# New costs and due times for a list scheduler that orders one stage of a kernel

## The chip, the cores and the metric

The kernel runs on one NeuronCore of a Trainium2 chip. Five instruction streams work side by side and meet only at semaphores: PE (TensorE, matrix products), DVE (VectorE), ACT (ScalarE), POOL (GpSimd) and SP (SyncE, which here only issues DMA transfers). Each engine takes its own instructions strictly in the order in which the program holds them. The metric is the device time of one execution in microseconds (us), median of several; lower is better.

## The reference

Three layers in a row, all in fp32 (shapes: 2 batches, 8 heads, 768 tokens, 64 wide; then 1536 tokens of 512).

```python
# attention, for each of the 16 (batch, head) pairs
q_bucket = sum(((q @ proj) > 0) * powers)        # 6 sign bits
k_bucket = sum(((k @ proj) > 0) * powers)
scores = where(q_bucket[:, None] == k_bucket[None, :], 0.125 * q @ k.T, -1e9)
attn = exp(scores - max(scores))
x = (attn / (attn.sum(-1) + 1e-9)) @ v
# dense layer: 512 -> 2048 -> 512 with mish, weights given in fp64
h = x @ w_in;  x = (h * tanh(softplus(h))) @ w_out
# eight experts: 512 -> 1024 -> 512 with relu, weighted by a Sinkhorn-normalised gate
out = sum_e P[:, e] * (relu(x @ w1[e]) @ w2[e])
```

## The kernel before, in words

**Stages.** `attention()` comes first, and then the two feed-forward layers as one long loop over 240 steps of matrix products. The change touches only `attention()`. To keep fp32 accuracy at the fast fp32r rate, operands are split into a high part (the fp32r rounding) and a low part (value minus high part), and products are sums of two or three fp32r products.

**Units of attention.** There are 16 heads `h`, each with two query blocks `u` (32 in all, 384 queries each). For one query block:

- `s_mm` (PE, tile `ps`, L369): three score tiles of 128 queries by 768 keys, with the bucket bits inside the product; `s_max` (DVE, `mx<-ps`, L383) takes each row's maximum. Only one `ps` buffer exists, so product and maximum alternate. `cols` (DVE, L388 and L391), `rows_mm` (PE, `prow`, L404) and `rows_cp` (ACT, `row`, L413) turn the maxima into rows that SP copies into place.
- For six key chunks `c`: `st_mm` (PE, `pst`, L421 and L422) makes transposed scores, `st_exp` (ACT, `p`, L427) their exponentials. Four of the six chunks are split: `split_hi` (`ph<-p`, through `copy`, L430) on ACT or DVE, `split_lo` (`plo<-p,ph`, through `subtract`, L433) on POOL. `av_mm` (PE, `pav`, L471) multiplies with the values; `av_count` (PE, `pav<-..,vf`, L456) opens each block's sum, so its row marks the start of a block's last part.
- `av_out` moves the sums out of PSUM (DVE `rs`, L479; ACT `xu`, L481). `norm` divides in five parts: reciprocals on DVE (L490, L493, L495), part 3 the product (`xu<-xu,rs`, L500, DVE), part 4 the high part (`xh`, L430), part 5 the low part (`xl`, L433).

For each head, `load_qk` and `load_v` bring data in, `prep_hi`, `prep_lo` and `prep_move` split it and SP moves the halves into the sets `sq`, `zq`, `ak`, `bk` (one of the three sets lies in the tile `wx`), `bits_*` (L306 to L327) make the bucket bits, `bits_fin` (`bit<-bit,cst`, L327, DVE) scales them.

**Decoding.** Between these, attention decodes the first four of the sixteen fp64 weight blocks, two chunks of 512 KB each: SP loads a chunk into a `stage` tile (three buffers, L105), then nine parts turn the fp64 bits into fp32 (DVE L119, L121, L127, L131, L135, L139; ACT L123, L125; POOL L141; DVE or POOL L143). `weight_hi` and `weight_lo` (L155, L160) split three finished blocks; the fourth is split when the feed-forward loop begins.

**What sets the order.** All of attention is a list of tasks. A task has an engine or a choice of engines with a cost each (`"A.42|D.27"`: ACT at 0.42 us or DVE at 0.27 us), a due time, and the tasks it comes after. When the program is built, a greedy list scheduler (the loop at the end of `attention()`) keeps a clock for each engine, takes the task with the least `start + DELTA * due`, and emits it. The costs and due times so decide the order on each engine and the engine of every task with a choice; at run time semaphores decide when anything starts. Chunk `n` of the decoding has the due time `DUE0 + PACE * n`, and a query block has `6 * u`.

Of the kernel before, what the change touches and what calls it, by code (L numbers as in the profile page):

```python
# [16 lines left out]
P = 128  # L17
B, H, S, D = 2, 8, 768, 64
# [4 lines left out]
E = 8  # L23
# [8 lines left out]
NSTAGE = 3  # L32
# [3 lines left out]
NP = 5  # L36
NPH = 3
WARM = 8
DELTA = 0.012
RECEIPT = 0.95  # L40
DIRECT = 2
DUE0 = 10
PACE = 11
# [14 lines left out]
def lsh_attention_moe_kernel(  # L58
# [108 lines left out]
    def attention():  # L167
        with ExitStack() as a:
# [370 lines left out]
            for h in range(NH):  # L539
# [5 lines left out]
                task("Q", 0.6 if h else 1.2, due - 24 if h else -99, load_qk, h, lag=1.1 if h else 0.55,  # L545
# [3 lines left out]
                for i in range(len(halves(h))):  # L549
                    task("A", 0.75 if h else 0.38, due - 14.0 if h else -50, prep_hi, h, i,  # L550
                         after=[nm(load_qk, h), *moved] + [nm(bits_mm, h - 1, j) for j in range(2) if h])
                    task("P1.8|D.87" if h else "D.5|", 0, due - 14.0 + 1 if h else -50, prep_lo, h, i, after=[his[i], *moved])
                for i in range(2):
                    task("E", 0.33, due - 10.0 + i, bits_mm, h, i, after=[los[i if h == 0 else 0], nm(proj_parts)], ring="m", frees=nm(bits_cmp, h, i))
                    task("A", 0.37, due - 10.0 + 0.5 + i, bits_corr, h, i,
                         after=[nm(bits_mm, h, i)] + ([nm(bits_cmp, *((h, 0) if i else (h - 1, h > 1)))] if h else []))
                    task("D", 0.47, due - 10.0 + 1 + i, bits_cmp, h, i, after=[nm(bits_corr, h, i)] + ([nm(bits_move, h - 1, j) for j in range(2)] if h > 1 else [nm(bits_fin, 0, j) for j in range(2)] if h else []))
# [23 lines left out]
                task("A0.38|D0.26", 0, vdue + 3, split_v, h, 0, after=[nm(load_v, h)] + freed[:1])  # L581
                task("P0.74|D0.34", 0, vdue + 4, split_v, h, 1, after=[nm(split_v, h, 0), nm(clear, "vh", h // 2 % 2), nm(clear, "vl", h // 2 % 2)])
# [3 lines left out]
            for u in range(NU):  # L586
                h, half = divmod(u, 2)
                due = 6 * u - 16.0
                for t in range(3):
                    before = nm(s_max, u, t - 1 - (u == 0 and t == 2)) if t else nm(s_max, u - 1, 2)  # L590
                    task("E", 0.33, due + 2 * t, s_mm, u, t,
                         after=[nm(prep_move, h, 0), nm(prep_move, h, 1), *([nm(bits_move, h, 0), nm(bits_move, h, 1)] if h else [nm(bits_fin, 0, 0), nm(bits_fin, 0, 1)])] + [before] * (u > 0 or t > 1))
                    task("D", 0.87, due + 2 * t + 0.5, s_max, u, t, after=[nm(s_mm, u, t)] + [nm(cols, u - 2)] * (t == 0 and u > 1))
                task("D", 0.15, due + 5, cols, u, after=[nm(s_max, u, t) for t in range(3)] + [nm(rows_mm, u - 2)] * (u > 1))
                direct = u < DIRECT
                task("E", 0.33 if direct else 0.11, due + 5.5, rows_mm, u, after=[nm(cols, u), nm(load_const, 2)] + [nm(warm_up)] * (u == 0), ring="m" if u else None, frees=nm(rows_cp, u))
                task("A", 0.37 if direct else 0.17, due + 6, rows_cp, u, after=[nm(rows_mm, u)] + [nm(rows_move, u - 1, t) for t in range(3) if u - 1 >= DIRECT])
# [7 lines left out]
                task("E", 0.17, 6 * u, av_count, u,  # L605
                     after=[nm(vsum_move, h | 1, j) for j in range(2)] + ready[:3] + ([nm(av_out, u - 2, 0), nm(av_out, u - 2, 1)] if u > 1 else [nm(s_max, 0, 1)]))
                for c in range(NKC):
                    i = 6 * u + c
                    sp = c in SPLIT
                    task("E", 0.33, i - 4.0, st_mm, u, c, after=ready + [nm(st_exp, *order[i - 2])] * (i > 1))  # L610
                    task("A", 0.38, i - 9.0, st_exp, u, c, after=[nm(st_mm, u, c)] + ([nm(split_lo if order[i - NP][1] in SPLIT else av_mm, *order[i - NP])] if i >= NP else []))
# [4 lines left out]
                    task("E", 0.5 if sp else 0.65, i + 1.0, av_mm, u, c,  # L616
# [73 lines left out]
            count = 0  # L690
            while count < len(tasks):
# [23 lines left out]
                free[e] = start + cost  # L715
                ends[k] = start + cost + LAT[e]
# [11 lines left out]
                count += 1  # L728

# [293 lines left out]
```

## Time and profile before

| what | value |
|---|---|
| median of three runs | 1633.51 us (1629.63 to 1634.22) |
| the profiled execution | 1629.05 us, its span 1627.3 us |
| attention in that span (to the first product of the feed-forward loop) | 0 to 301.8 us |
| feed-forward layers | 301.8 to 1627.3 us |
| busy share of the whole span | PE 98%, PE weight load 80%, DVE 41%, ACT 30%, POOL 27% |

The profile comes from one execution. "Busy" is the time in which at least one instruction of the engine was under way. Matmuls are pipelined, so a PE that is busy 90% of a stretch can still have room. 1.75 us lie between the profiled span and the execution's own time.

### The profile page before, as it was taken

The numbers are of one execution on the slowest core, as the hardware profiler recorded it, in microseconds if no ns is written. First come the engines' busy times: TensorE is split into PE (matmuls) and PEld (weight loads), VectorE is DVE, ScalarE is ACT, GpSimd is POOL, SyncE is SP. The second block draws the span as 40 slices with busy tenths as digits, with TensorE's granted clock in tenths as the row PEclk, the third lists the DMA queues.
The fourth block names the chain that finished last, engine by engine and source line by source line (L and its number), as shares of the span: only waits on it lengthen the run. The fifth ranks groups of instructions, "written<-read, shape, count | busy, mean of one in ns | idle before, by whom it ended". The sixth has DMA issues, their size and how long they took to land.

```text
span 1627.3 us, 18002 instructions
## 1 busy us (share of the span) xinstructions
PE 1588.7 (98%) x7071; PEld 1304.6 (80%) x7071; DVE 661.3 (41%) x1082; ACT 486.9 (30%) x866; POOL 446.0 (27%) x304
## 2 busy tenths in 40 slices
PE   6898999999999999999999999999999999999998
PEld 5677787788888878888888888888888888888887
DVE  8999988677883222332211111121212121212112
ACT  5666676544333322231121121121112112113110
POOL 5777766433333320130040031022012003004000
PEclk7999999999999999999999999999999999999999
DMA  7545442021212010030020021011012003002001
GB/s 184 136 122 146 112 117 53 27 72 58 68 63 78 2 51 0 13 91 0 1 91 13 1 69 35 0 52 53 0 28 77 1 13 91 1 0 65 15 12 52
DMA packets 40228, 83.94 MB, mean 52 GB/s; under 512 B 17280, under 2 KB 18024, under 8 KB 40144
## 3 DMA queue, kind: packets, MB, share of 16 engines
q1 hardware_dynamic: 40144, 82.80, 17.7%
q8 instruction: 55, 0.90, 0.2%
q14 instruction: 29, 0.24, 0.0%
HBM read 59.86 MB, written 3.15 MB: 39 GB/s over the span
## 4 chain that ended last, share of the span: by engine, by line
PE 87%; DVE 9%; issue 1%; DMA 1%; POOL 1%; ACT 0%; SPq 0%; DVEq 0%; POOLq 0%; ACTq 0%
PE y L805 40%; PE h L769 13%; PE h L771 13%; PE h L770 13%; PE pav L471 3%; DVE mx L383 2%; PE ps L369 1%; PE pst L421 1%; PE pst L422 1%; DVE vs L338 1%; DVE ph L430 1%; DMA wx<-hi 0%; DVE stage L135 0%; DVE rs L479 0%; DVE stage L127 0%
## 5 line engine op out<-in xcount | busy, mean ns | idle before, releaser
L786 DVE SCALAR_TENSOR_TENSOR gl<-h,gh 128x512 fp32r<-128x512 f32 x192 | 132.8, 692 | 805.4 <-ACT gh L785 805.4
L805 PE MATMUL y<-w,gh 128*128 128x512 f32 x1344 | 413.7, 389 | 0.0
L785 ACT ACTIVATE gh<-h 128x512 fp32r<-128x512 f32 x192 | 114.8, 598 | 867.0 <-PE h L771 867.0
L160 POOL TENSOR_TENSOR w<-stage,w 128x1024 fp32r<-128x1024 f32 x56 | 134.1, 2396 | 781.1 <-ACT w L155 781.1
L771 PE MATMUL h<-xh,w 128*128 128x512 f32 x840 | 326.9, 389 | 2.8 <-POOL w L160 2.8
L769 PE MATMUL h<-xh,w 128*128 128x512 f32 x840 | 328.1, 391 | 0.0
L770 PE MATMUL h<-xl,w 128*128 128x512 f32 x840 | 326.9, 389 | 0.0
L805 PEld LDWEIGHTS y<-w,gh 128*128 128x128 f32 x1344 | 252.4, 188 | 52.1
L805 PE MATMUL y<-w,gl 128*128 128x512 f32 x672 | 261.4, 389 | 0.0
L771 PEld LDWEIGHTS h<-xh,w 128*128 128x128 f32 x840 | 157.7, 188 | 36.1 <-POOL w L160 3.3
L770 PEld LDWEIGHTS h<-xl,w 128*128 128x128 f32 x840 | 157.8, 188 | 32.6
L769 PEld LDWEIGHTS h<-xh,w 128*128 128x128 f32 x840 | 157.6, 188 | 32.7
L433 POOL TENSOR_TENSOR plo<-p,ph 128x384 fp32r<-128x384 f32 x128 | 139.3, 1100 | 71.0 <-ACT ph L430 34.9
L805 PEld LDWEIGHTS y<-w,gl 128*128 128x128 f32 x672 | 126.2, 188 | 26.3
L805 PE MATMUL y<-gh,w 128*128 128x512 f32 x336 | 110.3, 389 | 0.0
L427 ACT ACTIVATE p<-pst 128x384 f32<-128x384 f32 x192 | 92.9, 488 | 51.0 <-PE pst L422 46.4
L383 DVE TENSOR_REDUCE mx<-ps 128x1 f32<-128x768 f32 x95 | 89.8, 945 | 13.1 <-PE ps L369 12.1
L141 POOL TENSOR_TENSOR stage<-stage,sgn 128x512 f32<-128x512 f32 x32 | 45.8, 1433 | 129.9 <-DVE sgn L139 54.8
L805 PEld LDWEIGHTS y<-gh,w 128*128 128x128 f32 x336 | 63.0, 188 | 13.1
L781 ACT ACTIVATE t<-h 128x512 f32<-128x512 f32 x48 | 28.7, 599 | 138.4 <-PE h L771 138.4
L805 PE MATMUL y<-gl,w 128*128 128x512 f32 x168 | 65.4, 389 | 0.0
L828 DVE SCALAR_TENSOR_TENSOR acc<-y,prob,acc 128x512 f32<-128x512 f32 x84 | 57.1, 743 | 7.5 <-PE y L805 7.5
(172 smaller groups left out, 1950.1 us busy)
## 6 DMA issues: line engine op xcount, KB each, us to landing
stage<-in_w_dram SPq DMA_DIRECT2D x96, 512.0 KB
raw<-in_qk_dram SPq DMA_DIRECT2D x13, 384.0 KB
wx<-hi SPq DMA_DIRECT2D x20, 192.0 KB
vt<-in_v_dram SPq DMA_DIRECT2D x16, 192.0 KB
out_dram<-acc SPq DMA_DIRECT2D x12, 256.0 KB
zq<-hi SPq DMA_DIRECT2D x11, 192.0 KB
ak<-hi SPq DMA_DIRECT2D x11, 192.0 KB
zq<-lo SPq DMA_DIRECT2D x11, 192.0 KB
```

The lines of the kernel that those rows point to most:

```text
L160: nc.gpsimd.tensor_sub(dst[:, 1, :], source(i), f32(dst[:, 0, :]))
L383: nc.vector.tensor_reduce(out=m[:, t:t + 1], in_=s_t[t][:, :, :HALF], axis=AX.XY, op=ALU.max)
L427: nc.scalar.activation(p_t[u, c], st_t.pop((u, c))[:, :HALF], AF.Exp, scale=0.125)
L433: (nc.gpsimd if e == "P" else nc.vector).tensor_sub(out, in0, in1)
L471: nc.tensor.matmul(av_t[u][:, :HALF], x.rearrange("p a d -> p (a d)"), y, start=False, stop=(c == NKC - 1 and n == len(pairs) - 1),)
L769: nc.tensor.matmul(t, wt[:, 0, f], xh[:, kc, c], start=(kc == 0), stop=False)
L770: nc.tensor.matmul(t, wt[:, 0, f], xl[:, kc, c], start=False, stop=False)
L771: nc.tensor.matmul(t, wt[:, 1, f], xh[:, kc, c], start=False, stop=(kc == KC - 1))
L785: nc.scalar.activation(hi, t, AF.Relu)
L786: nc.vector.scalar_tensor_tensor(out=lo, in0=t, scalar=0.0, in1=f32(hi), op0=ALU.max, op1=ALU.subtract)
L805: nc.tensor.matmul(yps[j], x, y, start=(head and m == 0), stop=(tail and m == 2))
L828: nc.vector.scalar_tensor_tensor(out=dst, in0=y, scalar=prob[:, i, e:e + 1], in1=dst, op0=ALU.mult, op1=ALU.add)
```

## The change

It replaces the scheduler's table and gives four tasks another choice of engines. The computation is the same.

- Nearly every cost is raised to a new number (an `s_max` from 0.87 to 0.95, `st_exp` from 0.38 to 0.49, `vsum_red` from 0.9 to 1.5, the DVE parts of decoding from 0.35 to 0.7 up to 0.6 to 1.0), and so are the times assumed for transfers. `DELTA`, the weight of due times, goes from 0.012 to 0.02.
- The eight decode chunks are due at 20, 42, ... 174 instead of 10, 21, ... 87 (query block 31 is due at 186). The first three loads of chunks must now wait for the moves of head 1.
- `split_hi` loses its choice: ACT does all 128. `bits_fin` and part 3 of `norm` get a choice of DVE or POOL.

```diff
-DELTA = 0.012
+DELTA = 0.02
-DUE0 = 10
-PACE = 11
+DUE0 = 20
+PACE = 22
...
-            def bits_fin(h, j):
+            def bits_fin(h, j, e):
...
-                nc.vector.tensor_scalar(
+                (nc.gpsimd if e == "P" else nc.vector).tensor_scalar(
...
-                    nc.vector.tensor_mul(xu[:, c], xu[:, c], rs[:, c])
+                    (nc.gpsimd if e == "P" else nc.vector).tensor_mul(xu[:, c], xu[:, c], rs[:, c])
...
-                    task("D", 0.53, due - 5.0, bits_fin, h, j, after=[nm(bits_cmp, h, 0), nm(bits_cmp, h, 1), nm(load_const, 1)]
+                    task("D.92|P1.2" if h else "D.67|", 0, due - 5.0, bits_fin, h, j, after=[nm(bits_cmp, h, 0), nm(bits_cmp, h, 1), nm(load_const, 1)]
...
-                        task("A.42|D.27", 0, i - 5.0, split_hi, u, c, after=[nm(st_exp, u, c)] + ([nm(av_mm, *k[-NPH])] if len(k) >= NPH else []))
-                        task("P.96|", 0, i - 1.0, split_lo, u, c, after=[nm(split_hi, u, c)])
+                        task("A", 0.51, i - 5.0, split_hi, u, c, after=[nm(st_exp, u, c)] + ([nm(av_mm, *k[-NPH])] if len(k) >= NPH else []))
+                        task("P1.12|", 0, i - 1.0, split_lo, u, c, after=[nm(split_hi, u, c)])
...
-                    task("D", 0.47, due, norm, u, 3, after=[nm(norm, u, 2)])
+                    task("D.83|P1.12", 0, due, norm, u, 3, after=[nm(norm, u, 2)])
...
-                task("Q", 0.6, due - 8, weight_load, n, after=[nm(decode, *divmod(n - NSTAGE, 2), 8)] if n >= NSTAGE else [], lag=1.45)
+                task("Q", 0.6, due - 8, weight_load, n, after=[nm(decode, *divmod(n - NSTAGE, 2), 8)] if n >= NSTAGE else [nm(prep_move, 1, j) for j in range(6)], lag=1.45)
...
-                costs = (("D", 0.35), ("A.67|D.33", 0), ("A", 0.67), ("D", 0.35), ("D", 0.45), ("D", 0.7), ("D", 0.4), ("P", 1.25), ("D.75|P1.2", 0))
+                costs = (("D", 0.6), ("A.67|D.6", 0), ("A", 0.68), ("D", 1.0), ("D", 0.6), ("D", 1.0), ("D", 0.6), ("P", 1.35), ("D.75|P1.1", 0))
```

What comes out, counted in the built programs: on DVE 42 `split_hi` casts are gone (ACT has 128 instead of 86), 7 of 15 `bits_fin` and 7 of 16 products of `norm` stand on POOL, and so do the `prep_lo` of heads 1 and 2. In return DVE takes two more decode sums (L143), two more `vl` and one more `xl` from POOL. PE and SP hold the same instructions in another order.

Three places show the order.

On DVE, between the `cols` of query blocks 6 and 7, the kernel before had two casts of `split_hi` (L430), a decode step (L135) and the product of `norm`:

```order
L430 CAST ph<-p 128x384
L383 TENSOR_REDUCE mx<-ps 128x1
L479 STREAM_TRANSPOSE rs<-pav 64x384
L433 TENSOR_TENSOR xl<-xu,xh 128x384
L383 TENSOR_REDUCE mx<-ps 128x1
L490 TENSOR_SCALAR nr<-rs 128x12
L493 RECIPROCAL nr<-nr 128x12
L430 CAST ph<-p 128x384
L495 STREAM_TRANSPOSE rs<-nr 128x384
L135 SCALAR_TENSOR_TENSOR stage<-stage,sgn_83 128x512
L383 TENSOR_REDUCE mx<-ps 128x1
L500 TENSOR_TENSOR xu<-xu,rs 128x384
```

The changed kernel has at the same place:

```order
L500 TENSOR_TENSOR xu<-xu,rs 128x384
L383 TENSOR_REDUCE mx<-ps 128x1
L479 STREAM_TRANSPOSE rs<-pav 64x384
L433 TENSOR_TENSOR xl<-xu,xh 128x384
L383 TENSOR_REDUCE mx<-ps 128x1
L490 TENSOR_SCALAR nr<-rs 128x12
L493 RECIPROCAL nr<-nr 128x12
L479 STREAM_TRANSPOSE rs<-pav 64x384
L383 TENSOR_REDUCE mx<-ps 128x1
L495 STREAM_TRANSPOSE rs<-nr 128x384
```

The casts and the decode step are gone from between the three maxima.

Later on DVE, between the `cols` of query blocks 23 and 24, the kernel before had no decoding any more:

```order
L479 STREAM_TRANSPOSE rs<-pav 64x384
L430 CAST ph<-p 128x384
L383 TENSOR_REDUCE mx<-ps 128x1
L321 TENSOR_TENSOR bit<-pbits,corr 44x384 x2
L383 TENSOR_REDUCE mx<-ps 128x1
L327 TENSOR_SCALAR bit<-bit,cst 44x768
L383 TENSOR_REDUCE mx<-ps 128x1
```

The changed kernel has three decode steps (L127, L131, L135) there, and no cast and no `bits_fin`:

```order
L383 TENSOR_REDUCE mx<-ps 128x1
L321 TENSOR_TENSOR bit<-pbits,corr 44x384
L127 TENSOR_SCALAR stage<-stage 128x512
L383 TENSOR_REDUCE mx<-ps 128x1
L321 TENSOR_TENSOR bit<-pbits,corr 44x384
L131 TENSOR_SCALAR stage<-stage 128x512
L383 TENSOR_REDUCE mx<-ps 128x1
L135 SCALAR_TENSOR_TENSOR stage<-stage,sgn_84 128x512
```

In the changed kernel a decode step follows each maximum here; the work of decoding now runs through to the last blocks.

On SP's queue at the start, `wx<-hi`, `wx<-lo` and `wx<-bit` are the moves of head 1 (one piece of the difference, - before, + after):

```order
 L222 DMA raw<-in_qk_dram 128x768
-L105 DMA stage<-in_w_dram 128x1024
 L228 DMA vt_127<-in_v_dram 128x6x64 x2
+L217 DMA wg<-in_wgate_dram 128x32
 L289 DMA wx_78<-hi 64x768 x4
 L289 DMA wx_78<-lo 64x768 x2
-L105 DMA stage<-in_w_dram 128x1024
-L217 DMA wg<-in_wgate_dram 128x32
+L289 DMA vf<-vsh 1x2x64
+L289 DMA vf<-vsl 1x2x64
 L289 DMA wx_78<-bit 12x768 x2
 L105 DMA stage<-in_w_dram 128x1024
```

Two weight loads that stood ahead of `wx<-bit` are now behind it, and the two small `vf` moves ahead of it.

## Rows read from the trace of the kernel before

**Rows 1.** Windows: busy time of each engine in five stretches, then clock and DMA.

```profile
core 0: us, PE busy (x) PEld busy (x) DVE busy (x) ACT busy (x) POOL busy (x), PEclk, DMA share, GB/s
0.00:27.60 27.60, 16.68 (x52) 11.99 (x52) 22.28 (x47) 15.12 (x28) 13.64 (x24) 0.77 0.95 235
27.60:203.30 175.70, 158.66 (x730) 125.69 (x729) 169.08 (x272) 118.37 (x257) 129.97 (x108) 0.97 0.47 125
203.30:284.10 80.80, 77.37 (x381) 64.10 (x380) 67.39 (x120) 56.53 (x126) 53.27 (x48) 1.00 0.33 86
284.10:301.80 17.70, 17.61 (x86) 14.54 (x85) 6.99 (x15) 12.26 (x28) 11.93 (x12) 1.00 0.01 2
301.80:1627.30 1325.50, 1318.38 (x5829) 1088.26 (x5827) 395.59 (x630) 284.59 (x430) 237.14 (x113) 1.00 0.12 37
```

**Rows 2.** Timeline of PE: start, us; `av_count` of blocks 0, 19, 29; feed-forward begins.

```profile
27.60 0.68 PE L456 MATMUL pav<-sq,vf 4*128 4x384 f32 x1
...
203.30 0.44 PE L456 MATMUL pav<-sq,vf 4*128 4x384 f32 x1
...
284.11 0.43 PE L456 MATMUL pav<-sq,vf 4*128 4x384 f32 x1
...
301.79 0.69 PE L769 MATMUL h<-xh,w 128*128 128x512 f32 x1
```

**Rows 3.** Waits of PE: who released it, us in total, times, longest.

```profile
PE prow L404 <- DVE col L391: 10.4, 11, 2.2
PE ps L369 <- DVE mx L383: 9.6, 17, 1.7
...
PE h L771 <- POOL w L160: 2.8, 1, 2.8
```

**Rows 4.** Windows of instructions on tile `stage` (decoding): the two middle stretches.

```profile
27.60:203.30 175.70, 39.67 (x48) 6.13 (x9) 12.91 (x10) 0.97 0.47 125
203.30:284.10 80.80, 0.00 (x0) 0.00 (x0) 0.00 (x0) 1.00 0.33 86
```

**Rows 5.** Groups of DVE instructions in 0 to 301.8: busy us, mean ns, idle before.

```profile
L383 DVE TENSOR_REDUCE mx<-ps 128x1 f32<-128x768 f32 x95 | 89.8, 945 | 13.1 <-PE ps L369 12.1
L430 DVE CAST ph<-p 128x384 fp32r<-128x384 f32 x42 | 22.2, 528 | 3.1 <-ACT p L427 1.7 <-PE pav L471 0.7
...
L327 DVE TENSOR_SCALAR bit<-bit,cst 44x768 fp32r<-44x768 f32 x15 | 13.1, 870 | 0.0
L500 DVE TENSOR_TENSOR xu<-xu,rs 128x384 f32<-128x384 f32 x15 | 12.3, 818 | 0.5
...
L433 DVE TENSOR_TENSOR xl<-xu,xh 128x384 fp32r<-128x384 f32 x6 | 6.4, 1070 | 0.1
...
L143 DVE TENSOR_TENSOR dec<-stage 128x512 f32<-128x512 f32 x6 | 4.4, 739 | 0.0
...
L433 DVE TENSOR_TENSOR vl<-vt,vh 128x256 fp32r<-128x256 f32 x4 | 1.6, 412 | 1.3 <-ACT vh L430 1.3
```

**Rows 6.** Groups of ACT and POOL instructions in 0 to 301.8, same columns.

```profile
L433 POOL TENSOR_TENSOR plo<-p,ph 128x384 fp32r<-128x384 f32 x128 | 139.3, 1100 | 71.0 <-ACT ph L430 34.9 <-DVE ph L430 29.8 <-DVE nr L490 6.0
...
L430 ACT CAST ph<-p 128x384 fp32r<-128x384 f32 x86 | 44.0, 512 | 6.5 <-PE pav L471 4.5
...
L433 POOL TENSOR_TENSOR lo<-raw,hi 128x768 fp32r<-128x768 f32 x12 | 23.1, 1921 | 0.7 <-ACT hi L280 0.7
```

**Rows 7.** Durations of three DVE forms in 0 to 301.8: ns min/median/max, first and last start.

```profile
L430 DVE CAST ph<-p x42: 308/358/2409, 20.1 to 299.5; 128x384 fp32r<-128x384 f32 x42
...
L500 DVE TENSOR_TENSOR xu<-xu,rs x15: 530/551/1591, 65.1 to 300.9; 128x384 f32<-128x384 f32 x15
...
L383 DVE TENSOR_REDUCE mx<-ps x95: 894/945/959, 12.7 to 285.5; 128x1 f32<-128x768 f32 x95
```

**Rows 8.** Chain that ended last, start us, us, what: two transfers at the start.

```profile
11.39 7.98 DMA wx<-hi
...
20.43 4.85 DMA wx<-bit
```

**Rows 9.** SP's issues of two weight loads, and of the bits between them and PE.

```profile
9.07 0.43 SPq L105 DMA_DIRECT2D stage<-in_w_dram  x1
...
16.79 0.33 SPq L105 DMA_DIRECT2D stage<-in_w_dram  x1
...
19.45 1.74 SPq L289 DMA_DIRECT2D wx<-bit  x2
```

More of the change, by code (lines that the diff above doesn't have):

```diff
@@ L549, in attention @@
                 for i in range(len(halves(h))):
-                    task("A", 0.75 if h else 0.38, due - 14.0 if h else -50, prep_hi, h, i,
+                    task("A", 0.84 if h else 0.5, due - 14.0 if h else -50, prep_hi, h, i,
                          after=[nm(load_qk, h), *moved] + [nm(bits_mm, h - 1, j) for j in range(2) if h])
-                    task("P1.8|D.87" if h else "D.5|", 0, due - 14.0 + 1 if h else -50, prep_lo, h, i, after=[his[i], *moved])
+                    task("P1.9|D.95" if h else "D.5|", 0, due - 14.0 + 1 if h else -50, prep_lo, h, i, after=[his[i], *moved])
                 for i in range(2):
-                    task("E", 0.33, due - 10.0 + i, bits_mm, h, i, after=[los[i if h == 0 else 0], nm(proj_parts)], ring="m", frees=nm(bits_cmp, h, i))
-                    task("A", 0.37, due - 10.0 + 0.5 + i, bits_corr, h, i,
+                    task("E", 0.35, due - 10.0 + i, bits_mm, h, i, after=[los[i if h == 0 else 0], nm(proj_parts)], ring="m", frees=nm(bits_cmp, h, i))
+                    task("A", 0.49, due - 10.0 + 0.5 + i, bits_corr, h, i,
                          after=[nm(bits_mm, h, i)] + ([nm(bits_cmp, *((h, 0) if i else (h - 1, h > 1)))] if h else []))
-                    task("D", 0.47, due - 10.0 + 1 + i, bits_cmp, h, i, after=[nm(bits_corr, h, i)] + ([nm(bits_move, h - 1, j) for j in range(2)] if h > 1 else [nm(bits_fin, 0, j) for j in range(2)] if h else []))
+                    task("D", 0.55, due - 10.0 + 1 + i, bits_cmp, h, i, after=[nm(bits_corr, h, i)] + ([nm(bits_move, h - 1, j) for j in range(2)] if h > 1 else [nm(bits_fin, 0, j) for j in range(2)] if h else []))
                 for j in range(6):
@@ L570, in attention @@
                 vdue = 12 * h - 12 * (h % 2) - 10.0
-                task("Q", 0.6, vdue - 10, load_v, h, after=freed + [nm(clear, "vt", h // 2 % 2)], lag=1.1)
+                task("Q", 0.6, vdue - 10, load_v, h, after=freed + [nm(clear, "vt", h // 2 % 2)], lag=2.0)
                 if h % 2:
                     first = h >= 3
-                    task("D", 0.9, vdue, vsum_red, h, after=[nm(load_v, h - 1), nm(load_v, h)] + [nm(vsum_mm, h - 2)] * first)
-                    task("E", 0.11, vdue + 1, vsum_mm, h, after=[nm(vsum_red, h), nm(clear_start)], ring="m", frees=nm(vsum_fin, h))
-                    task("D", 0.4, vdue + 2, vsum_fin, h, after=[nm(vsum_mm, h)] + [nm(vsum_move, h - 2, j) for j in range(2) if first])
+                    task("D", 1.5, vdue, vsum_red, h, after=[nm(load_v, h - 1), nm(load_v, h)] + [nm(vsum_mm, h - 2)] * first)
+                    task("E", 0.4, vdue + 1, vsum_mm, h, after=[nm(vsum_red, h), nm(clear_start)], ring="m", frees=nm(vsum_fin, h))
+                    task("D", 0.56, vdue + 2, vsum_fin, h, after=[nm(vsum_mm, h)] + [nm(vsum_move, h - 2, j) for j in range(2) if first])
                     for j in range(2):
@@ L590, in attention @@
                     before = nm(s_max, u, t - 1 - (u == 0 and t == 2)) if t else nm(s_max, u - 1, 2)
-                    task("E", 0.33, due + 2 * t, s_mm, u, t,
+                    task("E", 0.35, due + 2 * t, s_mm, u, t,
                          after=[nm(prep_move, h, 0), nm(prep_move, h, 1), *([nm(bits_move, h, 0), nm(bits_move, h, 1)] if h else [nm(bits_fin, 0, 0), nm(bits_fin, 0, 1)])] + [before] * (u > 0 or t > 1))
-                    task("D", 0.87, due + 2 * t + 0.5, s_max, u, t, after=[nm(s_mm, u, t)] + [nm(cols, u - 2)] * (t == 0 and u > 1))
-                task("D", 0.15, due + 5, cols, u, after=[nm(s_max, u, t) for t in range(3)] + [nm(rows_mm, u - 2)] * (u > 1))
+                    task("D", 0.95, due + 2 * t + 0.5, s_max, u, t, after=[nm(s_mm, u, t)] + [nm(cols, u - 2)] * (t == 0 and u > 1))
+                task("D", 0.45, due + 5, cols, u, after=[nm(s_max, u, t) for t in range(3)] + [nm(rows_mm, u - 2)] * (u > 1))
                 direct = u < DIRECT
-                task("E", 0.33 if direct else 0.11, due + 5.5, rows_mm, u, after=[nm(cols, u), nm(load_const, 2)] + [nm(warm_up)] * (u == 0), ring="m" if u else None, frees=nm(rows_cp, u))
-                task("A", 0.37 if direct else 0.17, due + 6, rows_cp, u, after=[nm(rows_mm, u)] + [nm(rows_move, u - 1, t) for t in range(3) if u - 1 >= DIRECT])
+                task("E", 0.4 if direct else 0.27, due + 5.5, rows_mm, u, after=[nm(cols, u), nm(load_const, 2)] + [nm(warm_up)] * (u == 0), ring="m" if u else None, frees=nm(rows_cp, u))
+                task("A", 0.47 if direct else 0.26, due + 6, rows_cp, u, after=[nm(rows_mm, u)] + [nm(rows_move, u - 1, t) for t in range(3) if u - 1 >= DIRECT])
                 ready = [nm(rows_cp, u)]
@@ L621, in attention @@
                 for j in range(2):
-                    task("DA"[j], (0.47, 0.38)[j], 6 * u + 10.0 + j / 2, av_out, u, j,
+                    task("DA"[j], (0.58, 0.47)[j], 6 * u + 10.0 + j / 2, av_out, u, j,
                          after=[nm(av_mm, u, NKC - 1)] + gone)
@@ L626, in attention @@
                     due = 6 * u + 14.0
-                    task("D", 0.35, due, norm, u, 1, after=both + ([nm(norm, u - 1 if half else u - 3, 2)] if u > 3 or half else []))
-                    task("D", 0.47, due, norm, u, 2, after=[nm(norm, u, 1)])
-                    task("D", 0.47, due, norm, u, 3, after=[nm(norm, u, 2)])
-                    task("A.42|" if u < NU - 1 else "D.27|", 0, due + 2, norm, u, 4, after=[nm(norm, u, 3)])
-                    task("P.96|D.47" if u < NU - 1 else "D.47|", 0, due + 3, norm, u, 5, after=[nm(norm, u, 4)])
+                    task("D", 0.72, due, norm, u, 1, after=both + ([nm(norm, u - 1 if half else u - 3, 2)] if u > 3 or half else []))
+                    task("D", 0.57, due, norm, u, 2, after=[nm(norm, u, 1)])
+                    task("D.83|P1.12", 0, due, norm, u, 3, after=[nm(norm, u, 2)])
+                    task("A.51|" if u < NU - 1 else "D.27|", 0, due + 2, norm, u, 4, after=[nm(norm, u, 3)])
+                    task("P1.12|D.9" if u < NU - 1 else "D.47|", 0, due + 3, norm, u, 5, after=[nm(norm, u, 4)])
             def weight_load(n):
@@ L689, in attention @@
                     offer(k)
-            count = 0
+            count, load = 0, {}
             while count < len(tasks):
@@ L715, in attention @@
                 free[e] = start + cost
+                load[e] = load.get(e, 0) + cost
                 ends[k] = start + cost + LAT[e]
@@ L728, in attention @@
                 count += 1
+            import os
+            if os.environ.get("SCHED"):
+                print("model end", max(ends.values()), {e: round(x, 1) for e, x in load.items()}, {e: round(x, 1) for e, x in free.items()})
     attention()
```

16 lines of the change are left out of this document (8 added, 8 removed).

## The prediction

> **What bounds the kernel now.** I read first the windows, cut where the timeline of PE shows a query block begin. Feed-forward takes 1325.5 us with PE busy 99.5% of it, and neither its products nor their order change, so everything has to happen in the first 301.8 us [rows 1, 2]. I cut those in four: a start (0 to 27.6), blocks 0 to 18 (175.7 us for 19 blocks, 9.25 us each), blocks 19 to 28 (80.8 us for 10, 8.08 us each) and a tail of 17.7 us. The reader should see two different limits there. In the first long stretch DVE is busy 169.08 of 175.7 us, 96%, while ACT is at 67% and POOL at 74%: DVE is full. In the second, DVE is at 83% and PE at 96%: PE is nearly full, and a block is 1.17 us faster. The windows of the tile `stage` say why: 39.67 us of decoding lie on DVE in the first stretch, none in the second [rows 4]. That is 2.09 us a block, and only 1.17 us come back when it ends, since PE then becomes the limit. The waits of PE agree: what it waits for, 10.4 us and 9.6 us in total, is the maxima and the columns that DVE makes [rows 3]. Over both stretches, 256.5 us and 29 blocks, a block costs 8.84 us.
>
> **The change part by part.** All DVE prices are means of the groups in attention [rows 5], contention included.
>
> *Taken off DVE.* The 42 casts cost 22.2 us; 36 to 37 of them lie in the two long stretches (the first begins at 20.1, the last at 299.5 [rows 7]); I take 19.4 us. Seven `bits_fin` at 870 ns are 6.1 us, seven products of `norm` at 818 ns 5.7 us. The two `prep_lo` fall mostly into the start; I count nothing for them. Coming back: two decode sums at 739 ns, two `vl` at 412, one `xl` at 1070, together 3.4 us. Net, 27.8 us less. DVE's 169.08 + 67.39 = 236.5 us become 208.7, or 7.20 us a block. If DVE were as full as in the first stretch, 96%, that would be 7.5 us a block: below the 8.08 that PE sets now. So DVE ceases to be the bound, provided that the work is spread; and it is, since decode steps now stand between the maxima of block 24 as well, where there were none.
>
> *Put on ACT.* The same 37 casts at 512 ns [rows 6] are 18.9 us. ACT's 118.37 + 56.53 = 174.9 us become 193.8, or 6.7 us a block.
>
> *Put on POOL.* The trace has no `bits_fin` and no product of `norm` on POOL. The product has the form of `plo`, two inputs of 128x384, so 1.10 us. For `bits_fin`, 768 wide with one input, the nearest rows are the same 1.10 us (half the width) below and `lo` with 1.92 us (768 wide, two inputs) above; I take 1.2 us, nearer to the one with as many elements read. Seven of each are 16.1 us; the five that leave POOL I don't deduct. POOL's 183.2 us become at most 199.3, or 6.9 us a block.
>
> *Moved: the rate that follows.* PE's own load is the same. In the second stretch it is busy 7.74 us a block, and that is the floor if every wait went. The row that resembles the new state most is that second stretch itself (no full DVE): 8.08 us. There ACT has 5.65 and POOL 5.33 us a block, and both will have over a microsecond more, in a chain that runs from `pst` through ACT, ACT, POOL to `pav`. I take 8.2 us a block for all 29. 29 x 8.2 = 237.8 us, 18.7 us less than 256.5. The bounds are 7.74 (224.5 us, 32 less) and 8.84 (nothing gained).
>
> *Moved: the start.* A chunk of 512 KB takes 2.2 us at the 235 GB/s of the start [rows 1]. Two of them were issued at 9.07 and 16.79, ahead of the bits of head 1 issued at 19.45 [rows 9], and the chain runs over just these: `wx<-hi` for 7.98 us and then `wx<-bit` for 4.85 [rows 8]. They now stand behind. That is between nothing, if the computed bits come no sooner, and 4.5 us; I take 2.5, about half. The loads don't vanish: three then go out in a row ahead of the moves of block 2's rows, 6.7 us of transfer, covered by blocks 0 and 1, which take more than 16 us. Without that cover 6.7 us would be lost.
>
> *The rest.* Raised costs and `DELTA` are no instructions; their price is the order, and it is in the rate. In the tail PE is busy 17.61 of 17.7 us; I leave it.
>
> Sum: 2.5 + 18.7 = 21.2 us off. The profiled execution took 1629.05 us, so 1607.9. The median shown is 4.5 us above that execution and the lowest run 0.6 us; I add 2 for a median: **1610 us**. The measurement tells a difference from none at about 0.3%, 4.9 us.
>
> **A rule that speaks against it.** The durations show DVE instructions stretched: the cast takes between 308 and 2409 ns, the product 530 to 1591 [rows 7], while the maximum, whose input is in PSUM, stays within 894 to 959. The Trainium skill, Perfetto Trace Analysis, section Optimizing Scalar/DVE Operations, says that where DVE is full some of its work may go to ScalarE or GpSimd, but that GpSimd shares a port with DVE, so that moving work between those two might not help. The trace agrees so far as the stretched durations go. By the rule the casts' move to ACT would count in full and the 14 instructions moved to POOL for nothing; what this makes of the time is the first rival.
>
> **The rivals.**
>
> *POOL's new work stands in DVE's way.* Suppose that each of the 16.1 us on POOL holds up DVE for its whole length, and that the waiting now in the casts, 42 x (528 - 308) ns = 9.2 us, passes to whatever comes next. DVE then has 208.7 + 25.3 = 234.0 us, 8.07 a block, and at 96% 8.4. 29 x 8.4 = 243.6, 12.9 less, with the start 15.4: about 1615 for a median (1613.7 + 2 = 1615.7). For it: the durations above. Against: in the second stretch POOL is busy 66% and DVE still has 17% idle.
>
> *PE alone is left.* 7.74 us a block and the whole 4.5 us of the start: 36.5 us less, 1594.6. For it: each of the other three engines has less than 7.3 us a block. Against: four engines in order, all above 85% of 7.74 us, need buffers of which `ps` has one.
>
> *Feed-forward waits for its weights.* PE waits 2.8 us there for a split now [rows 3]. The last chunk is decoded among the last blocks, and the next load needs its buffer. If one chunk's DVE work, 39.67 / 8 = 5.0 us, falls behind the end of attention, and its load of 2.2 us as well: 7.2 us back, 1617. Against: the last decode sum stands ahead of the last four `av_out` on DVE.
>
> *The order counts for nothing.* If waits in the chain of ACT and POOL keep the 8.84 us, only the start is left: 1629.05 - 2.5 + 2 = 1628.6. Against: the difference of the two stretches, which is DVE's.
>
> *Slower: ACT becomes the bound.* ACT works in order, and every cast now stands between two exponentials that PE waits for. In the second stretch ACT idles (80.8 - 56.53) / 10 = 2.43 us a block, in the first 3.02, waiting. Should that idle time remain and the casts simply be added, a block takes 6.7 + 2.43 = 9.13 us: 264.8, 8.3 more, less the start 5.8 more: 1634.9, or with 2 for the median 1637. It decides from 8.84 - 6.7 = 2.1 us of idle time on. For it: `plo` waits 34.9 us for ACT's casts already [rows 6], and buffers of `ph` are three. Against: it waits 29.8 us for DVE's casts too, 42 of them against 86, so a cast on the full DVE comes later than one on ACT.
>
> **How the numbers follow.** My forecast (1603 to 1613) gets 0.45, the port 0.15, PE alone 0.13, late weights 0.10, no effect 0.07, ACT 0.10. The range leaves out ACT's case and the better half of PE's, 16 to 17 in 100: 1596 to 1629. Faster by over 0.3%: 0.45 + 0.15 + 0.13 + 0.10 = 0.83; within 0.3%: 0.07; slower: 0.10.
>
> **What would show it.** Right: the first product of feed-forward starts at 280 (275 to 288) instead of 301.8; the busy share of DVE in any long stretch of attention stays under 92%; the blocks of the first half go from 9.25 to about 8.2 us and those of the second stay within 0.4 us of 8.08; `wx<-bit` lands before 23; 128 casts stand on ACT at 512 ns. The port's case would show as a mean of L500 and of the decode steps on DVE above theirs now; late weights as a wait of L771 over 2.8 us; ACT's case as PE waiting for `p` or `ph` for more than 30 us. A start of feed-forward after 300 would make the prediction wrong.

## The result: slower by 0.6%, and the profile after

The changed kernel takes 1642.62 us (median of four runs, 1640.7 to 1643.17) against 1632.83 us for the kernel before in the same comparison: a ratio of 1.0061, 95% interval 1.0043 to 1.0078. The forecast was 1610 us.

The windows of the changed kernel, cut where its query blocks begin as in [rows 1] (block 0, block 8, block 29, feed-forward); the profiled execution took 1643.17 us:

```profile
core 0: us, PE busy (x) PEld busy (x) DVE busy (x) ACT busy (x) POOL busy (x), PEclk, DMA share, GB/s
0.00:25.98 25.98, 16.60 (x52) 11.39 (x52) 21.95 (x41) 13.25 (x26) 14.85 (x24) 1.00 0.81 183
25.98:92.20 66.22, 63.34 (x307) 53.09 (x306) 55.86 (x93) 50.53 (x112) 47.16 (x41) 0.97 0.60 153
92.20:296.10 203.90, 177.07 (x803) 143.77 (x802) 174.74 (x250) 139.60 (x313) 153.89 (x126) 0.92 0.38 98
296.10:314.76 18.66, 17.96 (x85) 14.49 (x85) 9.32 (x19) 13.27 (x31) 14.14 (x13) 1.00 0.11 30
314.76:1641.40 1326.64, 1320.00 (x5829) 1089.42 (x5827) 395.99 (x629) 284.81 (x429) 237.06 (x113) 1.00 0.12 37
```

Feed-forward takes the same within 0.1%, but it starts at 314.76 instead of 301.79. Blocks 0 to 7 take 66.22 / 8 = 8.28 us each, nearly the 8.2 that was forecast, where the kernel before had 9.25 in its first long stretch. Then something begins: blocks 8 to 28 take 203.9 / 21 = 9.71 us each. No engine is full there (DVE 86%, PE 87%, POOL 75%, ACT 68%), and the granted clock of PE is 0.92 of full speed, against 0.97 in the blocks before. What begins at that point is in the durations of L327, the scaling of the bucket bits (ns min/median/max, first and last start):

```profile
L327 DVE TENSOR_SCALAR bit<-bit,cst x8: 660/766/1405, 21.5 to 211.6; 44x768 fp32r<-44x768 f32 x8
L327 POOL TENSOR_SCALAR bit<-bit,cst x7: 2918/2924/3369, 93.5 to 271.5; 44x768 fp32r<-44x768 f32 x7
```

The first of the seven on POOL starts at 93.5 us, in block 8. It takes 2.92 us at the median and 3.04 on average; the table says 1.2, and the prediction took 1.2. The groups of attention in the changed kernel, for those of [rows 5, 6]:

```profile
L433 POOL TENSOR_TENSOR plo<-p,ph 128x384 fp32r<-128x384 f32 x128 | 135.6, 1068 | 65.3 <-ACT ph L430 63.4 <-PE pav L471 0.9 <-DMA stage<-in_w_dram 0.8
L383 DVE TENSOR_REDUCE mx<-ps 128x1 f32<-128x768 f32 x95 | 90.1, 949 | 28.1 <-PE ps L369 26.8
L430 ACT CAST ph<-p 128x384 fp32r<-128x384 f32 x128 | 65.1, 510 | 17.0 <-PE pav L471 14.9 <-PE pst L422 0.8
L388 DVE TENSOR_SCALAR col<-mx 128x3 f32<-128x3 f32 x32 | 35.6, 1111 | 0.3
...
L327 POOL TENSOR_SCALAR bit<-bit,cst 44x768 fp32r<-44x768 f32 x7 | 21.3, 3042 | 1.2 <-DVE bit L321 1.1
...
L391 DVE TENSOR_SCALAR col<-mx 128x9 f32<-128x9 f32 x32 | 11.2, 351 | 0.0
...
L500 POOL TENSOR_TENSOR xu<-xu,rs 128x384 f32<-128x384 f32 x7 | 7.5, 1077 | 4.9 <-DVE rs L495 4.6 <-PE pst L422 0.3
```

The other prices were right: 510 ns for a cast on ACT, 1.08 us for a product on POOL. But L388, the first instruction of `cols` and a matter of 3 numbers in each partition, takes 1.11 us on average. Its durations, as ns min/median/max:

```profile
L388 DVE TENSOR_SCALAR col<-mx x32: 103/494/4958, 16.9 to 299.7; 128x3 f32<-128x3 f32 x32
```

The timeline around the second scaling on POOL shows the longest of them (start, us, engine, line):

```profile
116.68 3.09 POOL L327 TENSOR_SCALAR bit<-bit,cst 44x768 fp32r<-44x768 f32 x1
...
118.50 4.96 DVE L388 TENSOR_SCALAR col<-mx 128x3 f32<-128x3 f32 x1
...
119.37 4.10 DVE L391 TENSOR_SCALAR col<-mx 128x9 f32<-128x9 f32 x1
...
119.75 1.94 POOL L433 TENSOR_TENSOR plo<-p,ph 128x384 fp32r<-128x384 f32 x2
...
121.65 1.79 POOL L433 TENSOR_TENSOR lo<-raw,hi 128x768 fp32r<-128x768 f32 x1
123.40 0.99 POOL L433 TENSOR_TENSOR plo<-p,ph 128x384 fp32r<-128x384 f32 x1
...
123.53 0.38 PE L404 MATMUL prow<-idt,col 128*12 128x128 f32 x1 [3.31 <-DVE col L391]
...
124.03 0.52 PE L422 MATMUL pst<-sq,bk 100*128 100x384 f32 x1
```

POOL runs the scaling, two `plo` and a `lo` one behind the other without a gap, 6.8 us. DVE's L388 is issued at 118.50, while the scaling runs, and ends at 123.46, 0.02 us after the `lo`. It has been held through four POOL instructions. PE's next instruction is `rows_mm`, which needs the columns, and PE waits 3.31 us. After that its products take 0.52 us instead of 0.34: from 123.53 to 127 us the granted clock is 0.50 of full speed, the lower level. The waits of PE, for those of [rows 3]:

```profile
PE prow L404 <- DVE col L391: 15.0, 8, 3.3
PE ps L369 <- DVE mx L383: 9.5, 9, 4.1
...
PE h L776 <- POOL w L160: 2.8, 1, 2.8
PE prow L404 <- DVE mx L383: 2.3, 1, 2.3
...
PE pav L471 <- POOL plo L433: 1.3, 2, 0.7
```

At the start, the bits of head 1 are issued later than before, not sooner (22.23 us against 19.45 [rows 9]), and yet block 0 begins at 25.98 instead of 27.60:

```profile
22.23 1.57 SPq L289 DMA_DIRECT2D wx<-bit  x2
```

PE's first product on `wx`, in the kernel before and in the changed one, starts at nearly the same time:

```profile
25.41 0.98 PE L369 MATMUL ps<-wx 96*128 96x384 f32 x2 [2.22 <-DMA wx<-bit]
...
25.46 0.59 PE L369 MATMUL ps<-wx 96*128 96x384 f32 x2
```

In the kernel before two `pbits` and three `prow` products stand between it and the `av_count` of block 0, which starts 2.19 us later; in the changed one nothing does, and `av_count` starts 0.52 us later. So the 1.6 us come from PE's own order.

### The profile page after: what moved, and what is told of

Its sections match the earlier page's. It is cut to its first block, busy times and chain, and to the rows that moved or that the text cites. A ratio compares the mean times of both kernels' runs of the same rounds, so it can differ in the third digit from the quotient of the medians.

```text
span 1641.4 us, 18010 instructions
## 1 busy us (share of the span) xinstructions
PE 1595.0 (97%) x7071; PEld 1312.1 (80%) x7071; DVE 657.9 (40%) x1029; ACT 501.5 (31%) x908; POOL 467.1 (28%) x315
## 4 chain that ended last, share of the span: by engine, by line
PE 80%; DVE 0%; POOL 0%; ACT 0%; issue 0%
PE y L810 40%; PE h L774 13%; PE h L776 13%; PE h L775 13%; PE lg L844 0%; PE lt L855 0%; DVE acc L833 0%; POOL w L160 0%; PE pav L471 0%; PE cs L889 0%; ACT t L786 0%; PE mb L872 0%; PE mt L865 0%
## 5 line engine op out<-in xcount | busy, mean ns | idle before, releaser
L776 PE MATMUL h<-xh,w 128*128 128x512 f32 x840 | 327.5, 390 | 2.8 <-POOL w L160 2.8
L776 PEld LDWEIGHTS h<-xh,w 128*128 128x128 f32 x840 | 158.2, 188 | 36.2 <-POOL w L160 3.2
L433 POOL TENSOR_TENSOR plo<-p,ph 128x384 fp32r<-128x384 f32 x128 | 135.6, 1068 | 65.3 <-ACT ph L430 63.4
L383 DVE TENSOR_REDUCE mx<-ps 128x1 f32<-128x768 f32 x95 | 90.1, 949 | 28.1 <-PE ps L369 26.8
L786 ACT ACTIVATE t<-h 128x512 f32<-128x512 f32 x48 | 28.8, 599 | 140.0 <-PE h L776 140.0
L430 ACT CAST ph<-p 128x384 fp32r<-128x384 f32 x128 | 65.1, 510 | 17.0 <-PE pav L471 14.9
```

The lines of the kernel that those rows point to most:

```text
L383: nc.vector.tensor_reduce(out=m[:, t:t + 1], in_=s_t[t][:, :, :HALF], axis=AX.XY, op=ALU.max)
L430: nc.scalar.copy(out, in_) if e == "A" else nc.vector.tensor_copy(out, in_)
L433: (nc.gpsimd if e == "P" else nc.vector).tensor_sub(out, in0, in1)
L776: nc.tensor.matmul(t, wt[:, 1, f], xh[:, kc, c], start=False, stop=(kc == KC - 1))
```

## The experiments

Times are medians; the ratio to the kernel before from the same comparison stands in brackets with its interval. Line numbers in rows are those of each kernel.

**e1_fin_on_dve.** The order of the changed kernel, with the seven scalings issued to DVE.

```diff
-                (nc.gpsimd if e == "P" else nc.vector).tensor_scalar(
+                nc.vector.tensor_scalar(
                     out=(sq, bk)[j][0][64:76] if h == 0 else bit_t[0], in0=f32(bit_t[0])[r], ...
```

> The changed kernel with the order on every engine kept, but the seven scalings of bucket bits (bits_fin) that stood on POOL issued to DVE instead. Theory 1 (held port): DVE's small cols instruction cannot start while POOL runs instruction after instruction, and the 3.04 us scalings on POOL (1.2 us were assumed) make these runs long; expected mean of L388 on DVE from 1.11 to under 0.5 us, feed-forward starting near 290 instead of 315, time 1608 to 1625. Theory 2 (the order is bad: decoding among late blocks): DVE gets 6 us more, time 1638 to 1648. Theory 3 (ACT carries too much since all casts are on it): no change, 1638 to 1646.

1612.57 us (0.9892, 0.9869 to 0.9915): the one line is worth 28 us by the two ratios, 30 us by the two medians. The windows are cut at block 0, block 29 and feed-forward; the profiled execution, 1609.70 us, is the fastest of four:

```profile
0.00:25.00 25.00, 17.48 (x53) 12.23 (x53) 20.21 (x41) 13.37 (x26) 14.44 (x24) 1.00 0.86 197
25.00:264.60 239.60, 227.89 (x1110) 185.63 (x1109) 219.49 (x349) 189.44 (x425) 185.47 (x159) 1.00 0.49 125
264.60:282.90 18.30, 17.90 (x84) 14.48 (x84) 9.33 (x18) 13.22 (x31) 13.81 (x13) 1.00 0.11 30
```

29 blocks take 239.6 us, 8.26 each, the granted clock is 1.00, and feed-forward starts at 282.9. Against the changed kernel's 270.1 us for the same blocks (66.22 + 203.9) that is 30.5 us less: PE idles 11.7 us instead of 29.7, and is busy 227.9 instead of 240.4, at a higher clock. Its waits for the maxima and columns of DVE, listed below, sum to 10.5 us, against 26.8 in the changed kernel; those for POOL's `plo` go only from 1.3 to 0.4. So most of the 18.0 us of idle time that e1 saves was waiting for DVE, and not for POOL's own results:

```profile
PE prow L404 <- DVE col L391: 6.0, 8, 1.4
PE ps L369 <- DVE mx L383: 3.8, 8, 1.1
...
PE ps L369 <- DVE col L391: 0.7, 1, 0.7
```

L388 is held less, though its mean of 0.66 us is above the 0.5 that I expected:

```profile
L388 DVE TENSOR_SCALAR col<-mx x32: 121/554/2179, 15.3 to 268.2; 128x3 f32<-128x3 f32 x32
```

**e3_cols_reduce.** The held instruction itself in another form. Two tiles `mxs` hold the maxima beside a constant.

```diff
-                nc.vector.tensor_scalar(
-                    out=c[:, :, 0], in0=m, scalar1=-0.5 * BIG, scalar2=-1.0, op0=ALU.max, op1=ALU.mult
-                )
+                nc.vector.tensor_reduce(out=c[:, :, 0], in_=both, axis=AX.X, op=ALU.max, negate=True)
```

> The changed kernel with the first instruction of cols made a reduction over two columns (maximum and a constant, negated) instead of a tensor-scalar instruction; same result, same order, POOL unchanged. The maximum on L383, a reduction, never stretched (895 to 1002 ns). Theory 1: the reduction isn't held up, at most 0.3 us each instead of 1.11 us on average; feed-forward starts near 295, time 1612 to 1630. Theories 2 and 3: DVE saves its busy time, but PE goes on waiting, time 1636 to 1644.

1637.26 us (1.0041, 1.0028 to 1.0054): a miss. The groups say where the wait went (L392 and L393 are L388 and L391 of the changed kernel):

```profile
L393 DVE TENSOR_SCALAR col<-mxs 128x9 f32<-128x9 f32 x32 | 35.2, 1099 | 0.0
...
L392 DVE TENSOR_REDUCE col<-mxs 128x3 f32<-128x6 f32 x32 | 4.5, 141 | 0.3
```

The reduction is never held, as expected, but the tensor-scalar behind it is, for as long: 35.2 us now on the second instruction instead of 35.6 on the first. The trouble is not one unlucky instruction.

**e4_due_before** and **e5_cast_choice.** Two other parts of the change undone in the changed kernel, with the order made anew.

```diff
-DUE0 = 20
-PACE = 22
+DUE0 = 10
+PACE = 11
...
-                ... if n >= NSTAGE else [nm(prep_move, 1, j) for j in range(6)], lag=1.45)
+                ... if n >= NSTAGE else [], lag=1.45)
```

> The changed kernel with the due times and the gate of the decode chunks of the kernel before (10 + 11 n, no wait for the moves of head 1); costs and choices of engines as changed, so the order is made anew. Theory 2: decoding among the late blocks is what costs; time 1615 to 1632. Theories 1 and 3: the slow blocks move to the first half with the decoding, time 1636 to 1650.

```diff
-                        task("A", 0.51, i - 5.0, split_hi, u, c, ...
+                        task("A.51|D.36", 0, i - 5.0, split_hi, u, c, ...
```

> The changed kernel with the choice of DVE or ACT for the high parts of softmax given back (0.36 us on DVE, 0.51 on ACT), all else as changed; the order is made anew and 36 casts stand on DVE. Theory 3: ACT is relieved, PE waits less for p and ph, time 1618 to 1634. Theory 1: POOL still has 3.04 us scalings (3 of 15 here fewer or more do not matter), DVE has 36 more instructions that wait for the port, time 1640 to 1655. Theory 2: 1638 to 1650.

1641.17 us (1.0077, 1.0052 to 1.0102) and 1652.87 us (1.0136, 1.0100 to 1.0173). Neither edit wins the loss back. But the scheduler made the order anew and chose another number of scalings for POOL: six in e4 (3.16 us each) and eleven in e5 (2.95 us each), where the changed kernel has seven. (In e5, 38 casts came out on DVE, not 36.) So the extra time of e5 is not the price of the casts; e1_cast_choice below, without scalings on POOL, gives that.

**e2_fin_norm_dve.** The same single-line edit as in e1, for part 3 of `norm` too.

> As e1_fin_on_dve, and the seven products of norm that stood on POOL issued to DVE too, order kept. They took 1.08 us each on POOL and 0.94 on DVE. If POOL's load as such is what holds DVE up, 1604 to 1611; if only the 3 us scalings were the trouble, the same as e1 within 4 us (1609 to 1617).

1614.88 us (0.9898, 0.9881 to 0.9916), not told apart from e1. The seven products of 1.08 us on POOL cost nothing that can be measured, and bring nothing.

**e1_due_before** and **e1_cast_choice.** The edits of e4 and e5 made in e1.

> As e1_fin_on_dve with the due times and the gate of the decode chunks of the kernel before; order made anew. If spreading the decoding is worth what the prediction took (DVE full in the first half otherwise), 1618 to 1630; if the rest of the table does it, 1608 to 1616.

> As e1_fin_on_dve with the choice of DVE or ACT for the casts given back (36 on DVE); order made anew. If taking the casts off DVE is worth what the prediction took (19 us of DVE time), 1618 to 1630; if not, 1608 to 1616.

1625.42 us (0.9967, 0.9956 to 0.9978) and 1621.84 us (0.9943, 0.9925 to 0.9962). With the scalings off POOL, spreading the decoding is worth 12.9 us and taking the casts off DVE 9.3 us by medians, in orders made anew. Both parts save time, as the prediction argued. The pairs also price a scaling in these two orders: e4 is 15.8 us above e1_due_before with six on POOL, e5 31.0 us above e1_cast_choice with eleven, 2.6 and 2.8 us for each.

**d1_fin_dve_extra_pool.** Is it POOL that is in the way, or do the bits arrive too late when POOL scales them? All scalings on DVE as in e1, and an additional instruction on POOL at the seven places, on a tile of its own that nobody waits for.

```diff
+                if e == "P":
+                    nc.gpsimd.tensor_scalar(
+                        out=dum, in0=dum, scalar1=cst[0:44, 0:1], scalar2=cst[0:44, 1:2], op0=ALU.mult, op1=ALU.mult,
+                    )
```

> As e1_fin_on_dve (all scalings on DVE), plus an instruction of the same form as a scaling on POOL at the seven places where the changed kernel has one; it works on a tile that nobody else uses, so no data waits for it. Theory A (POOL's 3 us hold the port and POOL's own queue): the loss comes back, 1632 to 1646, with DVE instructions of 3 to 5 us again. Theory B (the bits themselves come too late when POOL scales them, and PE waits for them): it stays near e1, 1610 to 1620.

1627.75 us (0.9980, 0.9967 to 0.9992), between the two theories. It was not the same load, though: this instruction has the same shape, but takes 1.17 us. Even so its 8.2 us on POOL cost 15 us against e1.

```profile
L337 POOL TENSOR_SCALAR dum<-dum,cst 44x768 f32<-44x768 f32 x7 | 8.2, 1172 | 0.0
```

**d2_extra_pool_fp32r.** The same with subtraction and fp32r output, like a scaling.

```diff
-                        out=dum, in0=dum, scalar1=cst[0:44, 0:1], scalar2=cst[0:44, 1:2], op0=ALU.mult, op1=ALU.mult,
+                        out=dum, in0=f32(dum), scalar1=cst[0:44, 0:1], scalar2=cst[0:44, 3:4], op0=ALU.subtract, op1=ALU.mult,
```

> As d1_fin_dve_extra_pool, but the seven extra POOL instructions have the same operations and the fp32r output of a scaling (subtract, multiply, 44x768 fp32r from f32); in d1 (multiply, multiply, f32 output) they took 1.17 us, not 3.04. All scalings that count are on DVE. If form and output type set the length, they take about 3 us here. Theory A (POOL's long instructions hold DVE and POOL's own queue): most of the 30 us that e1 won are lost again, 1634 to 1648. Theory B (the bits come too late from POOL): at most what d1 lost, 1620 to 1630.

1640.76 us (1.0059, 1.0038 to 1.0081): nearly all of the 30 us is lost again.

```profile
L337 POOL TENSOR_SCALAR dum<-dum,cst 44x768 fp32r<-44x768 f32 x7 | 21.8, 3116 | 0.0
```

Nothing depends on these seven instructions. So the loss is POOL's time, and not the bits that come late. (Some 1.5 us of it lie ahead of block 0, which begins at 26.54 instead of 25.0.)

**d4_three_short_on_pool.** Three of d1's short instructions at each place.

> As d1_fin_dve_extra_pool with three of the short POOL instructions (1.17 us each, 3.5 us together) at each of the seven places instead of one. If it is the amount of POOL work at these places that costs, as much as or more than d2 with its single 3.1 us: 1638 to 1652. If it is the length of one instruction during which DVE cannot start, near d1: 1624 to 1634.

1642.16 us (1.0081, 1.0063 to 1.0098).

```profile
L338 POOL TENSOR_SCALAR dum<-dum,cst 44x768 f32<-44x768 f32 x21 | 25.2, 1200 | 1.4
```

Three short ones cost what one long one costs (25.2 us on POOL, 21.8 in d2). It is the amount of work that is put in a row at these places, not the length of one instruction.

**e9_f32_output.** What makes the scaling slow on POOL? First the output type.

```diff
-                    out=(sq, bk)[j][0][64:76] if h == 0 else bit_t[0], in0=f32(bit_t[0])[r], ...
+                    out=(sq, bk)[j][0][64:76] if h == 0 else f32(bit_t[0]), in0=f32(bit_t[0])[r], ...
```

> The changed kernel with one thing altered: the scalings write the same tile as f32 instead of fp32r (the values are exact in both). Seven stay on POOL, same order. If the fp32r output makes a POOL tensor-scalar long, they take 1.2 us, near the 1.2 us of the table, and the time falls to 1612 to 1625; if it is the subtraction, they stay at 3 us and the time at 1638 to 1646.

1641.92 us (1.0064, 1.0045 to 1.0084): unchanged, and so is the instruction.

```profile
L327 POOL TENSOR_SCALAR bit<-bit,cst 44x768 f32<-44x768 f32 x7 | 21.3, 3043 | 1.2 <-DVE bit L321 1.1
```

**f1_add_for_subtract.** Then the operation: the changed kernel, with a negated constant added.

```diff
-                    op0=ALU.subtract, op1=ALU.mult,
+                    op0=ALU.add, op1=ALU.mult,
```

> The changed kernel, same order, with the scaling written as an addition of the negated constant and a product instead of a subtraction and a product; the constants' table has the negated column. Seven stay on POOL. If the subtraction is what makes a POOL tensor-scalar of 44x768 take 3.04 us instead of 1.17, they take 1.2 us here, which is the table's price and the one that the prediction took, and the time is 1612 to 1626; if it is something else (the place of the tile, two constants per partition that differ), 3 us and 1638 to 1645.

1618.34 us (0.9920, 0.9902 to 0.9938), 24 us less than the changed kernel.

```profile
L327 POOL TENSOR_SCALAR bit<-bit,cst 44x768 fp32r<-44x768 f32 x7 | 7.5, 1065 | 1.2 <-DVE bit L321 1.1
```

With an addition it takes 1.07 us. This is the kernel that the prediction priced, and it falls 8 us above the forecast. Its windows, cut at block 0, block 29 and feed-forward (the profiled execution, 1620.71 us, is the slowest of four):

```profile
0.00:25.68 25.68, 16.99 (x53) 11.87 (x53) 21.39 (x41) 13.33 (x26) 14.82 (x24) 1.00 0.80 188
25.68:273.67 247.99, 229.53 (x1109) 188.23 (x1109) 222.58 (x343) 189.27 (x425) 190.79 (x166) 0.99 0.47 121
273.67:292.30 18.63, 17.93 (x85) 14.48 (x85) 9.30 (x19) 13.24 (x31) 14.12 (x13) 1.00 0.10 30
```

A block takes 247.99 / 29 = 8.55 us.

**p1_price_3us.** The changed kernel with the right price in the table (`"D.92|P3.04"`).

> The changed kernel with the cost of a scaling on POOL in the table raised from 1.2 to the measured 3.04 us; the scheduler still takes the engine that can start first, so 5 of 15 stay on POOL. If it is the wrong price that misled the order, the planned times of all that follows become right and the time falls to 1612 to 1625; if it is the instructions themselves, 5 of 7 remain and the time is 1628 to 1640.

1619.16 us (0.9924, 0.9904 to 0.9943). Five scalings of 3.03 us are still on POOL, and the kernel is 6.6 us above e1. That is 1.3 us for each, against 4.0 to 4.3 in the changed kernel and 2.6 and 2.8 in the orders of e4 and e5, all made with the wrong price. This speaks for the wrong price as the larger part of the loss, but p1 also has two scalings fewer and another order, so it is not shown by itself.

**b3_before_fin_pool.** The scalings of the same seven heads on POOL in the kernel before, nothing else.

> The kernel before with one part alone: the scalings of heads 6, 7, 8, 11, 13, 14 and 15 (the ones that the changed kernel gives to POOL) issued to POOL, order kept. If the scalings on POOL are what cost 30 us in the changed kernel, this costs some 15 to 35 us here, 1645 to 1665; if they only hurt in the new order, under 8 us, 1628 to 1639.

1645.79 us (1.0087, 1.0064 to 1.0110), 14.5 us more, at the lower end of what I had set. That is half of what they cost in the changed kernel; why only half, no run shows.

**e7_fin_dve_cols_reduce.** e1 and e3 together, the lowest median of the study.

> e1_fin_on_dve and e3_cols_reduce together: no scaling on POOL, and the first instruction of cols a reduction. In e1, L388 still takes 0.66 us on average, 21 us in all; in e3 the wait passed to the instruction behind it. If it passes on here too, the same as e1 within 5 us (1608 to 1617); if the short waits in e1 end with it, 1600 to 1608.

1608.50 us (0.9863, 0.9848 to 0.9877), 1.4% faster than the kernel before. It is 4.1 us below e1 by medians, inside the band in which I would have called the two equal.

## Why the prediction was wrong

**The step that failed** is one term: "For `bits_fin` ... I take 1.2 us". I had two rows, 1.10 and 1.92 us, and took both as bounds, but both are tensor-tensor instructions. The form was not in the trace. It measured 3.04 us, outside them; f1 shows the cause, the subtraction. So POOL got 21.3 + 7.5 = 28.8 us, not 16.1. f1, with the scaling at 1.07 us, puts 24 of the 33 us between forecast and measurement on this term. All that the seven scalings cost on POOL, by e1 and by d2 (seven such instructions without any effect on the data), is 28 to 30 us.

**What POOL's work does to DVE was put at nothing.** The sum counted the 16.1 us on POOL in POOL's own load alone, 6.9 us a block, below PE's. Yet 13.8 us of POOL work more than in f1 made 24 us of loss, through three steps that the profile shows one by one: POOL runs without a gap for 6.8 us; DVE's tensor-scalar instruction is held until the end of the fourth instruction (4.96 us at 118.50); PE, one `ps` buffer ahead, waits 3.31 us and then goes on at the lower clock. Between blocks 0 and 29, the profiled executions of the changed kernel and of e1 differ by 18.0 us of idle time of PE and by 12.5 us in which products take longer. The first rival named the mechanism and had 0.15, but its 1615.7 rests on the same 1.2 us, and it let each POOL instruction hold DVE for its own length only and did not speak of the clock. At its price it was nearer to f1's 1618.34 than the forecast; with 28.8 us in place of 16.1 its own sum gives 246.7 us of DVE work, 257.0 us for the blocks and about 1629, still 14 us too low. What the trace of before had was a cast held for 2.41 us [rows 7], by one instruction.

The Trainium skill, SBUF — State Buffer, section Who interferes with whom, says that of a two-port DVE instruction and a GpSimd instruction the one that issues first keeps the shared ports for its whole duration and the other is blocked, and that reductions never contend. The reduction agrees (141 ns on average in e3). The held instructions differ: L388 and L391 were not let in when the scaling ended but three POOL instructions later. That they are two-port instructions, no run here shows. What lets DVE in after some POOL instructions and not after others, the runs do not settle: in e1 POOL also runs without gaps, and L388 is held for 2.18 us at most.

**What held of the sum.** In e1 the start is 25.0 us (predicted 25.1), the blocks 8.26 us (8.2), feed-forward starts at 282.9 (280.6), and the time is 1612.6 (1610). But e1 is not the kernel that the prediction priced: its scalings are on DVE, 6 us that the sum had taken off. In f1, which is, the blocks take 8.55 us and feed-forward starts at 292.3, outside the 275 to 288 given as the sign of being right. The intervals of e1 and f1 overlap, and their profiles are the fastest and the slowest of four. So the second stretch of the kernel before was a fair row for the rate, but 8.2 us was somewhat low for this kernel, and that e1 comes within 3 us of the forecast is partly luck. Of the parts, decoding spread over all blocks measured 12.9 us and the casts on ACT 9.3 us. The start gained 1.6 us in the changed kernel, not 2.5, and for another reason: the bits of head 1 are issued until 23.8, after the 23 by which they were to land, and PE's first product with them starts no sooner (25.46, before 25.41); PE only has nothing left to do between it and block 0.

**The other rivals.** PE alone: not reached, 8.26 us a block even in e1, not 7.74. Late weights: the wait of L776 is 2.8 us as before. ACT as the bound: PE waits for `p` 0.8 us in all in the changed kernel, and e1_cast_choice loses 9.3 us by taking casts off ACT. "The order counts for nothing": refuted by e1, where a block takes 8.26 us and not 8.84.

## What to carry to other kernels

When an operation moves to an engine on which the trace has never shown it, bounds from neighbouring forms are no bounds: the operation itself (here subtract against add) can be worth a factor of 2.9, so measure that one instruction first. In a tight schedule (in e1 PE is busy 95% of the blocks and DVE 92%), a few microseconds that the plan does not know of can cost more than their length: here 13.8 us cost 24, since the queues run in order and PE came out of a wait of 3.31 us at half its clock. Made anew at the right price, the order kept five of the seven scalings on POOL and lost 6.6 us. And a mean busy share hides this: no engine of the slow stretch was above 87%.

## What was not expected of the hardware

- A tensor-scalar on GpSimd, 44 partitions by 768, takes 3.04 us with subtract and multiply, 1.07 with add and multiply, and 1.17 with two multiplies. The output type (fp32r or f32) makes no difference (3042 and 3043 ns).
- A DVE tensor-scalar of three elements in each partition was held for 4.96 us, through four GpSimd instructions in a row, one of 128x512 for 5.70 us; a DVE reduction of nearly the same operands took 141 ns on average at the same place (e3).
- With seven such scalings, 21 us of GpSimd time, TensorE idled 26.8 us of the 204 us of blocks 8 to 28, in waits of up to 4.1 us, and its granted clock there was 0.92. In the profiled execution of e1, without them, it idled 11.7 of 239.6 us, and the granted clock was 1.00.
